# Moving one batch's attention from the first layer's blocks into a phase of the second layer

## The chip, the cores and the metric

One core of one Trainium2 chip. The engines are PE (TensorE, matmuls; PEld is its weight load), DVE (VectorE), ACT (ScalarE), POOL (GpSimd) and SP (SyncE, which issues most DMAs here). The metric is the device time of one execution in microseconds, the median of several.

## The reference

Linear attention with a root-mean-square norm, and two MLPs behind it:

```python
batch, n_heads, seq, head_dim = (8, 8, 576, 64)
kv = np.einsum('bhsd,bhse->bhde', k, v)
out = np.einsum('bhsd,bhde->bhse', q, kv)
rms = np.sqrt(np.mean(out * out, axis=-1, keepdims=True) + 1e-06)
x = out / rms * g_norm                  # to (4608, 512): tokens x (heads * head_dim)
h = x @ w_in                            # (512, 2048)
g = where(h >= 1, h, where(h <= -1, 0, (h + 1) ** 2 / 4))
x = g @ w_out                           # (2048, 512)
h = x @ moe2_w_in
r = np.maximum(h, 0.0)
y = (r * r) @ moe2_w_out
```

## The kernel before

Every fp32 product of the MLPs is made of three matmuls on operands split into a high and a low part (fp32r). Tokens are worked on in blocks of 512, one block for each batch, and the 64 tokens left over of each batch make one block more.

**The plain phase** (to 631 us) does the first layer's blocks 0 to 4 whole and the first contraction of blocks 5 and 6, in steps of one of 16 column groups: `h_stage`, `g_stage` and `out_stage` (`mm3`, L246; activation at L723 and L725). Attention of the later batches is woven into it by `hook(slot, function)`: two slots to a step. For a batch `b` and a pair of heads `hp`, `load_kv` and `load_q` fetch, `kv_stage` makes k'v (`pkv`, L484) and copies it into `kvbd`, `t_stage` transposes q, `o_stage` multiplies (`po`, L588) and squares, and `r_stage` sums the squares (`pr`, L613), forms the reciprocal root on ACT (Ln, Exp, square) and DVE (`newton`, L527) and writes x. `STARTS` gives each pair's slot. The four pairs of batch 7 (`LAST_B`) stand among those of batches 4 to 6; their x is kept in DRAM (`xpd`, `xrd`) for later. Weight preparation is woven in as well: `prep_load`, `prep_narrow`, `prep_join`, `prep_sums`, `prep_split` at the slots of `SECOND` and `FIRSTS`, with the results stored in `wsd`.

**The pair phases** take two blocks at a time through both contractions with seven products in place of eight (`PRODUCTS`, order 1, 6, 2, 7, 5, 4, 3). `PAIRS` lists layer and first block: pair 0 is (layer 1, block 5), pair 1 is (layer 2, block 0), pair 2 is (2, 2), pair 3 is (1, 7), and so on. `in_phase(n)` is pair n's first contraction: four quarters of seven products, 28 steps of 12 matmuls (L924). Product 1 opens accumulators `x`, product 6 `y`, product 5 `z`; products 2, 7, 4 and 3 add onto a bank that has been read before. Banks are read by additions with earlier results, the `e` tiles: product 6 and 7 at L974, products 5, 4 and 3 at L981, with `{5: 7, 4: 1, 3: 6}` naming the `e` tile that each needs. `out_phase(n)` is the second contraction: 56 steps of 6 matmuls, whose operand `prepare` splits into a `t` tile (ACT, then DVE at L853); it reads its banks in the same way. `load_w2` fetches one 512 KB piece of weights for each 12 matmuls, on SP.

Buffers are handed round by `Ring`: a list of (pool, tag) places taken in turn. A tile of a tag waits until one of the tag's buffers has been freed by all who use it. Of those that matter here: tag `g` has three buffers (pool `gp`); `t_ring` is three times `g` and `w0_14`, `w0_15`; `e_ring` is `wk0`, `wk1`, `wk2`, `hl0`, `hl1` and `q`; `ps_ring` are the eight accumulator banks, two `at`, two `h`, four `acc`. Attention uses `at`, `q`, `wk0` to `wk2`, `hl0` and `hl1`.

A finished pair of layer 2 is written by `put_out`, four times, during the next pair's `in_phase`, at its steps 0, 1, 5 and 9 (`late`): DVE transposes (L1131) into a tile `ov` out of `t_ring`, then eight stores on SP (L1119). The order on each engine is set when the program is built: in program order, except that what can't start yet by the builder's own estimate is passed by what can.

Of the kernel before, what the change touches and what calls it, by code (L numbers as in the profile page):

```python
# [76 lines left out]
def linear_attention_rms_two_mlps(  # L77
# [12 lines left out]
    nc = tc.nc  # L90
# [15 lines left out]
    PACE = 0.75  # L106
    WAVE = 6
    WHOLE = ((1, 0), (1, 1))
    STARTS = (32, 39, 46, 53, 60, 66, 72, 78, 84, 90, 96, 102, 109, 115, 121, 127, 133, 139)
    STARTS += (145, 151, 156, 161, 166, 173)  # L110
    SECOND = (38, 47, 55.6, 64.2, 72.8, 84, 92.6, 101.2, 109.8, 119.8, 128.4, 137, 145.6)
    SECOND += (154.2, 166.8, 172.8)
    FIRSTS = (
        (44, 70.2, 78.8, 98.6, 107.2, 134.4, 143, 160.2),
        (81.4, 53, 117.2, 151.6, 90, 61.6, 125.8, 164.2),
    )
    WARMS = ((0, 5), (6, 5), (8, 3), (12, 4), (14, 3), (20, 3), (26, 3))
    SPLITS = (10, 15, 24, 29, 32, 33)
# [20 lines left out]

    PLAIN = 5  # L140
    PAIRS = [(1, PLAIN), (2, 0), (2, 2), (1, B - 1), (2, 4), (2, 6)]
    LAST_B = B - 1

    xpd = dr.tile([P, KD, TB], F32, name="xpd")
# [16 lines left out]
    def keep_halves(L, which, i, n, t, now=False):  # L161

        made = MADE[which][2 * n : 2 * n + 2]
        hs = slice(0, 2)
        if L == 1 and None in made and not (which == 1 and i + n * NH >= NF - TAIL):
            hs = slice(1, 2) if made[0] is None else slice(0, 1)
        dst = wsd[L, which, i // 2][:, 2 * n + hs.start : 2 * n + hs.stop, i % 2]
        if now:
            nc.sync.dma_start(dst, t[:, hs])
        else:  # L170
            owe(2, dst, t[:, hs])
# [15 lines left out]

    def split_halves(t, src, hi, lo):

        src = src.rearrange("p (h f) -> p h f", h=2)  # L190
        copy(hi, t[:, :, 0, :], src)
        lo.tensor_tensor(t[:, :, 1, :], src, t[:, :, 0, :].bitcast(F32), ALU.subtract)  # L192

# [179 lines left out]
    def prep_split(L, which, i, n):  # L373
        src = prep.pop((L, which, i, n))
        t = prep_tile(f"s{L}_{which}_{i}_{n}", [P, 2, 2, H2], F32R)
        split_halves(t, src, engine2("s_hi"), engine2("s_lo"))
        keep_halves(L, which, i, n, t.bitcast(F32))

    def keep_first(which, f):
# [31 lines left out]
    def load_kv(b, hp):  # L411
        h0 = 2 * hp
        if b > 0:

            r = rests[turn[b, hp] % len(rests)]
            kvr[b, hp] = (r[:, 0], r[:, 1])
        for n, src in enumerate((k, v)):
            pool, tag = (ep, "e") if (b, hp) == (0, NP - 1) else (st, "st")
            t = pool.tile([P, TB], F32, tag=tag, name=f"{'kv'[n]}_{b}_{hp}")
            rows = src[b, h0 : h0 + 2, :TB, :].rearrange("h (p r) d -> p h r d", r=MR)  # L420
            if n == 0:

                t = t.rearrange("p (r h d) -> p r h d", h=2, r=MR)
                nc.sync.dma_start(t, rows.rearrange("p h r d -> p r h d"))
            else:
                t = t.rearrange("p (h r d) -> p h r d", h=2, r=MR)
                nc.sync.dma_start(t, rows)
            kvm.setdefault((b, hp), []).append(t)
            if b > 0:
                rest = src[b, h0 : h0 + 2, TB:, :].rearrange("h p d -> p h d")  # L430
                nc.sync.dma_start(kvr[b, hp][n][:REM], rest)
# [169 lines left out]
    def r_stage(b, hp):  # L601
        (y, o), _ = hl.pop((b, hp))
        if (b, hp) in WHOLE:
            products = [(ones.bitcast(F32), y)]
        else:
            products = [(ones, s2) for s2 in og.pop((b, hp))]
        ms = []
        for half in range(2):
            c = slice(half * U, (half + 1) * U)
            ps = bank(b, f"pr_{b}_{hp}_{half}")  # L610
            m = ps[:, :U]
            for n, (one, s2) in enumerate(products):
                nc.tensor.matmul(m, one, s2[:, c], start=n == 0, stop=n == len(products) - 1)  # L613
            nc.scalar.activation(y[:, c], m, AF.Ln, bias=lnb, scale=LN_SCALE)
            ms.append((c, m))
        nc.scalar.activation(y, y, AF.Exp, bias=expb, scale=-0.5)
        t = ap1.tile([P, S], F32, tag="wk2", name=f"t_{b}_{hp}")
        square(engine("y", b), t, y)
        for c, m in ms:
            newton(t[:, c], m)  # L620
        if b < LAST_B:
            norm(t, y, o)
            nc.gpsimd.tensor_copy(xrem[b][:, hp, :], t[:, TB:])
            split(xs[1, b][hp], t[:, :TB], "x", b)
            return
        xt = st.tile([P, TB], F32, tag="st", name=f"xt_{hp}")
        nc.vector.scalar_tensor_tensor(t, t, -3.0, y, op0=ALU.add, op1=ALU.mult)
        nc.vector.tensor_tensor(xt, o[:, :TB], t[:, :TB], ALU.mult)
        xr = ap1.tile([P, REM], F32, tag="xr", name=f"xr_{hp}")
        nc.vector.tensor_tensor(xr, o[:, TB:], t[:, TB:], ALU.mult)  # L630
        x_kept[hp] = xt, xr

    x_kept = {}

    def keep_x(b, hp):
        xt, xr = x_kept.pop(hp)
        nc.sync.dma_start(xpd[:, hp, :], xt)
        nc.sync.dma_start(xrd[:, hp, b, :], xr)

    def new_x(L, b):  # L640
        xs[L, b] = [
# [23 lines left out]
    def attention(starts, order):  # L665

        slots = []
        for j, (s, (b, hp)) in enumerate(zip(starts, order)):
            turn.setdefault((b, hp), len(turn))
            if b == 1:  # L670
                slots += [(max(0, s - 7), load_kv, b, hp), (s, kv_stage, (b, hp))]
            elif j % 2 == 0:
                two = order[j : j + 2]
                turn[two[1]] = len(turn)
                slots += [(max(0, s - 7), load_kv, *i) for i in two]
                slots.append((s, kv_stage, *two))
            slots += [
                (max(0, s - 7), load_q, b, hp),
                (s, t_stage, b, hp),
                (s + 3, o_stage, b, hp, 0),  # L680
                (s + 4, o_stage, b, hp, 1),
            ]
            if hp == 0 and b < LAST_B:
                slots.append((s + 6, begin, b))
            slots.append((s + 6, r_stage, b, hp))
            if b == LAST_B:
                slots.append((s + 8, keep_x, b, hp))
            elif hp == NP - 1:
                slots.append((max(2 * NF * b, 0) if b < PLAIN + 1 else s + 9, store_xrem, b))
        return slots  # L690

# [126 lines left out]
    )  # L818
    e_ring = Ring(*((ap1, t) for t in ("wk0", "wk1", "wk2", "hl0", "hl1")), (ap2, "q"))
    t1_ring = Ring(*[(st, "st")] * 7, (dt, "dt3"))  # L820
    v_ring = Ring(*((wp, f"w0_{i}") for i in (12, 13)))
    tmp = Ring(*[(ep, "e"), (dt, "dt0"), (ep, "e"), (dt, "dt1"), (ep, "e"), (dt, "dt2")])
    ps_ring = Ring(*[(ps_t, "at")] * 2, *[(ps_h, "h")] * 2, *((ps_a, f"acc{c}") for c in range(KD)))
# [96 lines left out]
    def mm_group(ps, lhs, rhs, first, last):  # L920

        for n, (wt, xt) in enumerate(zip(lhs, rhs)):
            for i, (a, c) in enumerate(((0, 0), (0, 1), (1, 0))):
# [6 lines left out]
                    skip_group_check=True,  # L930
                )

    FIRST = (1, 6, 5)
    bank_of = {1: "x", 2: "x", 6: "y", 7: "y", 4: "y", 5: "z", 3: "z"}
    g2 = {}
# [2 lines left out]
    def in_phase(n):  # L938
# [6 lines left out]
        for q in range(NQ):  # L945
            ps = {}
            e = {}
            for p in PRODUCTS:
                w = take_w2(layer(n), 0, q, p)
                for i in range(2):  # L950
# [9 lines left out]
                        True,  # L960
                    )
                    if p == 1:
                        e[i, 1] = tile(e_ring, f"e1_{n}_{k}")
                        g2[k] = [
                            g_ring.tile([P, 2, N], F32, f"g2_{n}_{k}_{j}") for j in range(2)
                        ]
                        nc.scalar.copy(e[i, 1], bank)
                    elif p in (6, 7):
                        kind = "e16" if p == 6 else "e167"
                        if p == 6:  # L970
                            e[i, 6] = tile(e_ring, f"{kind}_{n}_{k}")
                        else:
                            e[i, 7] = tile(e_ring, f"{kind}_{n}_{k}")
                        nc.vector.tensor_tensor(e[i, p], bank, e[i, 1], ALU.add)  # L974
                    else:
                        g = g2[k][0 if p in (2, 3) else 1][:, {2: 0, 3: 1, 4: 0, 5: 1}[p], :]
# [176 lines left out]

    jobs = [(8, store_xrem, 0)]
    jobs += attention((0, 7, 14, 21), [(1, hp) for hp in range(NP)])
    order = []
    for b in range(2, LAST_B):
        order += [(LAST_B, b - 4)] * (b >= 4) + [(b, hp) for hp in range(NP)]
    order.append((LAST_B, NP - 1))
    jobs += attention(STARTS, order)  # L1160
    for job in sorted(jobs, key=lambda j: j[0]):
        hook(*job)
    for i in range(NF):
# [25 lines left out]
    for which in range(2):  # L1189
        for i, t in enumerate(FIRSTS[which]):  # L1190
            parts += [
                (t, prep_join, 1, which, i),
                (t + 1, prep_sums, 1, which, i),
                (t + 1, prep_split, 1, which, i, 2),
                (t + 2, prep_split, 1, which, i, 3),
            ]
    for t, *part in sorted(parts, key=lambda p: p[0]):
        hook(int(t), *part)
# [83 lines left out]
    late = []  # L1282
    rows_left = []

    for n in range(NS + 1):
        step_in = in_phase(n) if n else ()
        for i, _ in enumerate(step_in):
            pay(True)
            if late and i in (0, 1, 5, 9) and n < NS:
                late.pop(0)()  # L1290
# [8 lines left out]
            late.pop(0)()  # L1299
        if n == NS:  # L1300
            break
        result[n] = result_of(dict(g2))
        steps = start_out(n) if n else out_steps[0]
        if n < NS - 1:
            for _ in steps:
                pay(True)
            if n == 0:
                w_ring.slots = [(wp, t) for t in ("w1_14", "w1_15", "w0_0", "w0_1")]
                w_ring.slots += [(wp, f"w1_{i}") for i in range(4)]
# [53 lines left out]
```

## Time and profile before

| what | value |
|---|---|
| median of 3 runs | 1556.14 us (1555.7 to 1557.11) |
| the profiled execution | 1555.4 us |
| its span, first to last instruction | 1553.6 us |
| PE, DVE, ACT busy | 1542.2, 1143.3, 970.6 us |
| matmuls in the trace | 7633 |
| moved by DMA | 369.27 MB, mean 238 GB/s |

The plain phase takes the first 631 us. Pair 0's `out_phase` follows; the `in_phase` of pairs 1, 2 and 3 starts at 707, 860 and 1012 us, each some 76 us long, with an `out_phase` of the same length behind it. Busy time of PE is modelled from pipelined matmuls: a matmul's record is longer than the time until the next one starts, so counts over a stretch say more than durations.

### The profile page before, as it was taken

How to read it: one execution, taken by the hardware profiler on the slowest of the kernel's cores; microseconds unless marked ns; L12 is line 12 of the kernel's file. 1: busy time of each engine (PE TensorE's matmuls, PEld its weight loads, DVE VectorE, ACT ScalarE, POOL GpSimd, SP SyncE). 2: the span in 40 equal slices, each digit the busy share in tenths (PEclk: the TensorE clock that was granted, in tenths of full speed). 3: DMA queues.
4: the chain of work that ended last, by engine and by line, in shares of the span. 5: the costliest groups of instructions: out<-in, count | busy, mean ns of one | idle time of the engine just before them, and what ended most of it. 6: DMA issues, size and time to landing. Idle time of an engine off the chain costs nothing.

```text
span 1553.6 us, 22167 instructions
## 1 busy us (share of the span) xinstructions
PE 1542.2 (99%) x7633; PEld 1273.5 (82%) x7633; DVE 1143.3 (74%) x1991; ACT 970.6 (62%) x1833; POOL 15.1 (1%) x38
## 2 busy tenths in 40 slices
PE   9999999999999999999999999999999999999999
PEld 5787888878878888888888888888888888888899
DVE  6986787787878766984597559778965597558666
ACT  5977676667767667654575466456646664666374
POOL 0000000000000000000000000000000000000000
PEclk9999999999999999999999999999999999999999
DMA  9666899989897945586576867696876676977796
GB/s 290 189 223 187 260 328 292 294 269 289 255 300 214 293 156 179 185 262 216 164 246 197 228 210 248 197 226 212 258 227 205 199 245 196 241 249 213 223 393 249
DMA packets 324479, 369.27 MB, mean 238 GB/s; under 512 B 197008, under 2 KB 222608, under 8 KB 324368
## 3 DMA queue, kind: packets, MB, share of 16 engines
q1 hardware_dynamic: 293472, 311.75, 67.0%
q10 hardware_dynamic: 30896, 56.11, 9.7%
q8 instruction: 61, 1.00, 0.3%
q14 instruction: 50, 0.41, 0.1%
HBM read 283.64 MB, written 84.15 MB: 237 GB/s over the span
## 4 chain that ended last, share of the span: by engine, by line
PE 97%; ACT 1%; DVE 1%; issue 0%; DVEq 0%; ACTq 0%
PE po L924 32%; PE ph L924 27%; PE ph L246 19%; PE acc L246 14%; PE po L588 1%; PE pkv L484 1%; PE pr L613 1%; PE pwarm L1218 1%; ACT raw L276 0%; ACT w L225 0%; PE pr L542 0%; DVE t L527 0%; DVE w L192 0%; PE po L519 0%; ACT u L232 0%; DVE t L530 0%
## 5 line engine op out<-in xcount | busy, mean ns | idle before, releaser
L924 PE MATMUL po<-t,ws 128*128 128x512 f32 x2016 | 458.1, 389 | 0.0
L924 PEld LDWEIGHTS po<-t,ws 128*128 128x128 f32 x2016 | 378.3, 188 | 78.9 <-DVE t L853 0.3
L924 PE MATMUL ph<-x,ws 128*128 128x512 f32 (+1 forms) x2016 | 422.1, 371 | 0.0
L924 PEld LDWEIGHTS ph<-x,ws 128*128 128x128 f32 x2016 | 355.8, 188 | 65.6
L246 PE MATMUL ph<-x,w 128*128 128x512 f32 x1344 | 335.0, 396 | 3.5 <-DVE u L725 2.2
L246 PEld LDWEIGHTS ph<-x,w 128*128 128x128 f32 x1344 | 249.0, 188 | 60.6 <-DVE u L725 4.3
L853 DVE TENSOR_TENSOR t<-g,t 128x512 fp32r<-128x512 f32 (+1 forms) x336 | 216.3, 649 | 91.6 <-ACT t L225 85.8
L225 ACT CAST t<-g 128x512 fp32r<-128x512 f32 (+1 forms) x336 | 195.3, 590 | 119.3 <-PE po L924 60.8
L981 DVE TENSOR_TENSOR h<-ph,e 128x512 f32<-128x512 f32 (+1 forms) x144 | 93.0, 646 | 68.3 <-PE ph L924 60.5
L246 PE MATMUL acc<-gs,w 128*128 128x512 f32 x528 | 134.4, 396 | 1.5 <-DVE u L725 1.5
L246 PEld LDWEIGHTS acc<-gs,w 128*128 128x128 f32 x528 | 97.9, 188 | 22.6 <-DVE u L725 2.0
L246 PE MATMUL acc<-gs,wt 128*128 128x512 f32 x432 | 108.5, 395 | 0.0
L988 ACT ACTIVATE h<-h 128x512 f32<-128x512 f32 (+1 forms) x120 | 70.2, 585 | 60.2 <-DVE h L981 55.3
L974 DVE TENSOR_TENSOR e<-ph,e 128x512 f32<-128x512 f32 (+1 forms) x96 | 61.0, 644 | 51.6 <-PE ph L924 50.8
L246 PEld LDWEIGHTS acc<-gs,wt 128*128 128x128 f32 x432 | 80.3, 188 | 17.0
L725 DVE SCALAR_TENSOR_TENSOR u<-u,ph 128x512 f32<-128x512 f32 x80 | 54.4, 680 | 30.8 <-ACT u L232 30.8
L225 ACT CAST x<-xr 128x512 fp32r<-128x512 f32 (+1 forms) x84 | 48.7, 585 | 43.3 <-DVE xr L904 21.8
L225 ACT CAST gs<-u 128x512 fp32r<-128x512 f32 x80 | 49.8, 622 | 38.6 <-DVE u L725 31.7
L989 ACT ACTIVATE g<-h 128x512 f32<-128x512 f32 (+1 forms) x120 | 70.7, 589 | 3.2
L723 ACT ACTIVATE u<-ph,halfb 128x512 f32<-128x512 f32 x80 | 55.2, 690 | 26.1 <-PE ph L246 21.8
L238 DVE TENSOR_TENSOR gs<-u,gs 128x512 fp32r<-128x512 f32 x80 | 54.9, 686 | 14.6 <-ACT gs L225 14.2
L988 ACT ACTIVATE u<-ph 128x512 f32<-128x512 f32 (+1 forms) x40 | 22.1, 552 | 62.7 <-PE ph L924 61.8
(144 smaller groups left out, 1603.7 us busy)
## 6 DMA issues: line engine op xcount, KB each, us to landing
ws<-wsd SPq DMA_DIRECT2D x364, 512.0 KB, 4.3
wsd<-s ACTq DMA_DIRECT2D x96, 512.0 KB, 4.7
wt<-wsd SPq DMA_DIRECT2D x36, 512.0 KB, 5.6
raw<-in_moe_w_in_dram SPq DMA_DIRECT2D x32, 512.0 KB, 5.9
raw<-in_moe_w_out_dram SPq DMA_DIRECT2D x32, 512.0 KB, 6.6
xr<-x1d SPq DMA_DIRECT2D x36, 256.0 KB, 4.7
out_dram<-ov SPq DMA_DIRECT2D x142, 64.0 KB, 3.8
wsd<-w SPq DMA_DIRECT2D x17, 512.0 KB, 4.6
```

The lines of the kernel that those rows point to most:

```text
L225: return e.copy(dst, src)
L238: lo = engine(op + "_lo", phase).tensor_tensor(t[:, 1, :], src, t[:, 0, :].bitcast(F32), ALU.subtract)
L246: nc.tensor.matmul(dst, wt(a), xt(c), start=first and n == 0, stop=last and n == 2)
L484: nc.tensor.matmul(ps[s, d], lhs, rhs, start=c == 0, stop=c == MR)
L723: nc.scalar.activation(u, ps, AF.Relu, bias=halfb, scale=0.5)
L725: nc.vector.scalar_tensor_tensor(u, u, 1.0, ps, op0=ALU.min, op1=ALU.max)
L853: engine2(op + "_lo").tensor_tensor(t[:, 1, :], src, t[:, 0, :].bitcast(F32), ALU.subtract)
L924: nc.tensor.matmul(ps, wt(a), xt(c), start=first and n == 0 and i == 0, stop=last and n == len(lhs) - 1 and i == 2, skip_group_check=True,)
L974: nc.vector.tensor_tensor(e[i, p], bank, e[i, 1], ALU.add)
L981: nc.vector.tensor_tensor(h, bank, add, ALU.add)
L988: nc.scalar.activation(u, h, AF.Relu)
L989: nc.scalar.activation(g, u, AF.Square)
```

## The change

Batch 7's four pairs leave the plain phase and run in `in_phase(2)`, at its steps 2, 8, 14 and 20 (`in_host`, `host`), their first loads during the `out_phase` before it (negative steps). For that phase `ps_ring` gives up the two `at` banks and gets them back in front of the list behind it; the `e` tiles, two at a time, go to tag `g` (`keep_e`, `e_pairs`) so that attention has `wk*`, `hl*` and `q`; k and v of pairs 2 and 3 go to `w0_14` and `w0_15` (`kv_ring`). x of batch 7 is made in place in `o` and stored at once from there. `STARTS`, `SECOND` and `FIRSTS` are spread anew over the slots. `prep_split` and `keep_halves` leave out weight quarters that no product reads (None in `MADE`).

```diff
-    STARTS = (32, 39, 46, 53, 60, 66, 72, 78, 84, 90, 96, 102, 109, 115, 121, 127, 133, 139)
-    STARTS += (145, 151, 156, 161, 166, 173)
-    SECOND = (38, 47, 55.6, 64.2, 72.8, 84, 92.6, 101.2, 109.8, 119.8, 128.4, 137, 145.6)
-    SECOND += (154.2, 166.8, 172.8)
+    STARTS = (32, 39, 46, 53, 61, 68, 75, 82, 92, 99, 106, 113, 122, 129, 136, 143)
+    STARTS += (151, 156, 161, 166)
+    SECOND = (37, 46, 55.2, 64.6, 73.2, 85, 93.6, 102.2, 110.8, 120.4, 128.8, 137.4, 146)
+    SECOND += (155, 167.6, 173.6)
...
+    HOST = 2
...
-        if L == 1 and None in made and not (which == 1 and i + n * NH >= NF - TAIL):
+        if None in made and not (L == 1 and which == 1 and i + n * NH >= NF - TAIL):
...
-        split_halves(t, src, engine2("s_hi"), engine2("s_lo"))
+        made = MADE[which][2 * n : 2 * n + 2]
+        hs = [h for h in range(2) if made[h]]
+        src = src[:, hs[0] * H2 : (hs[-1] + 1) * H2]
+        split_halves(t[:, hs[0] : hs[-1] + 1], src, engine2("s_hi"), engine2("s_lo"))
...
+        both = None
+        if b == LAST_B and hp > 1:
+            both = kv_ring.tile([P, 2, TB], F32, f"kv_{b}_{hp}")
...
-        xt = st.tile([P, TB], F32, tag="st", name=f"xt_{hp}")
         nc.vector.scalar_tensor_tensor(t, t, -3.0, y, op0=ALU.add, op1=ALU.mult)
-        nc.vector.tensor_tensor(xt, o[:, :TB], t[:, :TB], ALU.mult)
-        xr = ap1.tile([P, REM], F32, tag="xr", name=f"xr_{hp}")
-        nc.vector.tensor_tensor(xr, o[:, TB:], t[:, TB:], ALU.mult)
-        x_kept[hp] = xt, xr
...
+        nc.vector.tensor_tensor(o, o, t, ALU.mult)
+        nc.sync.dma_start(xpd[:, hp, :], o[:, :TB])
+        nc.sync.dma_start(xrd[:, hp, b, :], o[:, TB:])
...
-                (max(0, s - 7), load_q, b, hp),
+                (max(0, s - 7) if b < LAST_B else s - 5, load_q, b, hp),
...
+    kv_ring = Ring(*((wp, f"w0_{i}") for i in (NF - 2, NF - 1)))
+    e_pairs = Ring(*[(gp, "g")] * 3)
+    banks_at = [(ps_t, "at")] * 2
...
+    def keep_e(n, e, i, p, k):
+
+        if n != HOST:
+            e[i, p] = e_ring.tile([P, TB], F32, f"e{p}_{n}_{k}")[:, : width(n)]
+        elif i == 0:
+            t = e_pairs.tile([P, 2, TB], F32, f"e{p}_{n}_{k}")
+            e[0, p], e[1, p] = t[:, 0], t[:, 1]
...
-    order = []
-    for b in range(2, LAST_B):
-        order += [(LAST_B, b - 4)] * (b >= 4) + [(b, hp) for hp in range(NP)]
-    order.append((LAST_B, NP - 1))
-    jobs += attention(STARTS, order)
+    jobs += attention(STARTS, [(b, hp) for b in range(2, LAST_B) for hp in range(NP)])
+    in_host = {}
+    for at, *job in attention((2, 8, 14, 20), [(LAST_B, hp) for hp in range(NP)]):
+        in_host.setdefault(at, []).append(job)
...
+    def host(i):
+        for at in sorted(a for a in in_host if a <= i):
+            for f, *a in in_host.pop(at):
+                f(*a)
...
+        if n == HOST:
+            ps_ring.slots = [a for a in ps_ring.slots if a not in banks_at]
         for i, _ in enumerate(step_in):
+            if n == HOST:
+                host(i)
             pay(True)
             if late and i in (0, 1, 5, 9) and n < NS:
                 late.pop(0)()
...
+        if n == HOST:
+            host(7 * NQ)
+            ps_ring.add(*banks_at)
...
-            for _ in steps:
+            for i, _ in enumerate(steps):
                 pay(True)
+                if n == HOST - 1 and i % 2 == 0:
+                    host(i // 2 - 7 * NQ)
```

## Rows read from the trace of the kernel before

**Rows 1.** The page, busy us of each engine, share of the span, instructions.
```profile
PE 1542.2 (99%) x7633; PEld 1273.5 (82%) x7633; DVE 1143.3 (74%) x1991; ACT 970.6 (62%) x1833; POOL 15.1 (1%) x38
```
**Rows 2.** Windows: PE, PEld, DVE, ACT, POOL busy (count), granted clock, DMA share, GB/s.
```profile
330.00:430.00 100.00, 98.42 (x540) 80.64 (x539) 79.41 (x145) 69.46 (x145) 1.81 (x4) 1.00 0.87 271
430.00:530.00 100.00, 98.89 (x539) 80.64 (x538) 75.37 (x137) 69.10 (x145) 2.09 (x4) 1.00 0.87 269
...
650.00:700.00 50.00, 50.00 (x222) 41.39 (x222) 44.16 (x72) 28.35 (x49) 0.00 (x0) 1.00 0.81 255
...
860.00:936.00 76.00, 76.00 (x337) 62.94 (x336) 43.30 (x66) 44.34 (x74) 0.00 (x0) 1.00 0.78 220
944.00:984.00 40.00, 40.00 (x178) 33.10 (x178) 39.63 (x66) 24.89 (x46) 0.00 (x0) 1.00 0.72 215
```
**Rows 3.** Groups by line, PE, 130 to 631 us: busy, mean ns, idle before, releasers.
```profile
L246 PE MATMUL ph<-x,w 128*128 128x512 f32 x1144 | 284.3, 396 | 2.2 <-DVE u L725 2.2
...
L588 PE MATMUL po<-qT,kvbd 128*128 128x288 f32 x96 | 29.0, 405 | 0.5 <-ACT kvbd L225 0.5
L484 PE MATMUL pkv<-v,k 128*64 128x64 f32 x384 | 15.3, 225 | 0.0
L613 PE MATMUL pr<-s,ones 128*128 128x288 f32 x48 | 14.2, 301 | 0.0
L613 PE MATMUL pr<-s2lo,ones 128*128 128x288 f32 x48 | 11.3, 296 | 0.0
L484 PE MATMUL pkv<-rest 128*64 128x64 f32 x96 | 6.9, 222 | 0.0
```
**Rows 4.** Timeline, 341 to 346 us: start, us, instruction [idle before, its releaser].
```profile
341.85 0.87 ACT L225 COPY kvbd<-pkv 64x64 f32<-64x64 f32 x4 [5.08 <-PE pkv L484]
...
345.94 0.73 PE L246 MATMUL ph<-x,w 128*128 128x512 f32 x2 [1.58 <-DVE u L725]
```
**Rows 5.** Timeline of DVE around the start of the phase that will host.
```profile
854.71 2.67 DVE L1131 STREAM_TRANSPOSE ov<-g 128x512 f32<-128x512 f32 x4
...
869.67 0.69 DVE L974 TENSOR_TENSOR e<-ph,e 128x512 f32<-128x512 f32 x1
```
**Rows 6.** Timeline of PE: first rows of this phase and of the next.
```profile
859.95 2.43 PE L924 MATMUL ph<-x,ws 128*128 128x512 f32 x10
...
936.11 10.14 PE L924 MATMUL po<-t,ws 128*128 128x512 f32 x44
```
**Rows 7.** Timeline of SP's issues, 853 to 900 us.
```profile
855.46 0.69 SPq L1119 DMA_DIRECT2D out_dram<-ov  x1
...
863.25 4.01 SPq L1119 DMA_DIRECT2D out_dram<-ov  x5
...
868.02 5.65 SPq L1119 DMA_DIRECT2D out_dram<-ov  x8
873.77 3.02 SPq L840 DMA_DIRECT2D ws<-wsd  x4
```
**Rows 8.** Tile `ov`, 850 to 905 us: its stores, issue to landing.
```profile
DMA to landing us min/median/max: 2.0/3.9/6.4
```
**Rows 9.** Timeline, 332 to 340 us: the last `pr` of a pair and its `newton`.
```profile
332.08 0.43 PE L613 MATMUL pr<-s2lo,ones 128*128 128x288 f32 x2
...
338.58 0.82 DVE L527 SCALAR_TENSOR_TENSOR t<-pr,t 128x288 f32<-128x288 f32 x2
```
**Rows 10.** Groups by line and form, whole span: `r_stage` behind `pr`.
```profile
L614 ACT ACTIVATE wk<-pr,lnb 128x288 f32<-128x288 f32 x56 | 27.3, 503 | 13.6 <-PE pr L613 13.6
L527 DVE SCALAR_TENSOR_TENSOR t<-pr,t 128x288 f32<-128x288 f32 x64 | 26.4, 452 | 11.7 <-ACT t L232 9.3 <-issue 2.2
...
L616 ACT ACTIVATE wk<-wk,expb 128x576 f32<-128x576 f32 x28 | 22.0, 785 | 0.2
...
L232 ACT ACTIVATE t<-wk 128x576 f32<-128x576 f32 x28 | 19.1, 684 | 0.3
```

More of the change, by code (lines that the diff above doesn't have):

```diff
@@ L108, in linear_attention_rms_two_mlps @@
     WHOLE = ((1, 0), (1, 1))
-    STARTS = (32, 39, 46, 53, 60, 66, 72, 78, 84, 90, 96, 102, 109, 115, 121, 127, 133, 139)
-    STARTS += (145, 151, 156, 161, 166, 173)
-    SECOND = (38, 47, 55.6, 64.2, 72.8, 84, 92.6, 101.2, 109.8, 119.8, 128.4, 137, 145.6)
-    SECOND += (154.2, 166.8, 172.8)
+    STARTS = (32, 39, 46, 53, 61, 68, 75, 82, 92, 99, 106, 113, 122, 129, 136, 143)
+    STARTS += (151, 156, 161, 166)
+    SECOND = (37, 46, 55.2, 64.6, 73.2, 85, 93.6, 102.2, 110.8, 120.4, 128.8, 137.4, 146)
+    SECOND += (155, 167.6, 173.6)
     FIRSTS = (
-        (44, 70.2, 78.8, 98.6, 107.2, 134.4, 143, 160.2),
-        (81.4, 53, 117.2, 151.6, 90, 61.6, 125.8, 164.2),
+        (42.6, 70.2, 78.8, 99.2, 107.8, 134.4, 143, 160.6),
+        (81.4, 52, 117.4, 151.6, 90.6, 60.9, 126, 164.6),
     )
@@ L188, in split_halves @@
     def split_halves(t, src, hi, lo):
-        src = src.rearrange("p (h f) -> p h f", h=2)
+        src = src.rearrange("p (h f) -> p h f", f=H2)
         copy(hi, t[:, :, 0, :], src)
@@ L416, in load_kv @@
             kvr[b, hp] = (r[:, 0], r[:, 1])
+        both = None
+        if b == LAST_B and hp > 1:
+            both = kv_ring.tile([P, 2, TB], F32, f"kv_{b}_{hp}")
         for n, src in enumerate((k, v)):
-            pool, tag = (ep, "e") if (b, hp) == (0, NP - 1) else (st, "st")
-            t = pool.tile([P, TB], F32, tag=tag, name=f"{'kv'[n]}_{b}_{hp}")
+            if both is not None:
+                t = both[:, n, :]
+            else:
+                pool, tag = (ep, "e") if (b, hp) == (0, NP - 1) else (st, "st")
+                t = pool.tile([P, TB], F32, tag=tag, name=f"{'kv'[n]}_{b}_{hp}")
             rows = src[b, h0 : h0 + 2, :TB, :].rearrange("h (p r) d -> p h r d", r=MR)
@@ L625, in r_stage @@
             return
-        xt = st.tile([P, TB], F32, tag="st", name=f"xt_{hp}")
         nc.vector.scalar_tensor_tensor(t, t, -3.0, y, op0=ALU.add, op1=ALU.mult)
-        nc.vector.tensor_tensor(xt, o[:, :TB], t[:, :TB], ALU.mult)
-        xr = ap1.tile([P, REM], F32, tag="xr", name=f"xr_{hp}")
-        nc.vector.tensor_tensor(xr, o[:, TB:], t[:, TB:], ALU.mult)
-        x_kept[hp] = xt, xr
[L633 to L638, printed above, removed]
+        nc.vector.tensor_tensor(o, o, t, ALU.mult)
+        nc.sync.dma_start(xpd[:, hp, :], o[:, :TB])
+        nc.sync.dma_start(xrd[:, hp, b, :], o[:, TB:])
     def new_x(L, b):
@@ L674, in attention @@
                 turn[two[1]] = len(turn)
-                slots += [(max(0, s - 7), load_kv, *i) for i in two]
+                slots += [(s - 7, load_kv, *i) for i in two]
                 slots.append((s, kv_stage, *two))
             slots += [
-                (max(0, s - 7), load_q, b, hp),
+                (max(0, s - 7) if b < LAST_B else s - 5, load_q, b, hp),
                 (s, t_stage, b, hp),
@@ L685, in attention @@
             slots.append((s + 6, r_stage, b, hp))
-            if b == LAST_B:
-                slots.append((s + 8, keep_x, b, hp))
-            elif hp == NP - 1:
+            if b < LAST_B and hp == NP - 1:
                 slots.append((max(2 * NF * b, 0) if b < PLAIN + 1 else s + 9, store_xrem, b))
@@ L962, in in_phase @@
                     if p == 1:
-                        e[i, 1] = tile(e_ring, f"e1_{n}_{k}")
+                        keep_e(n, e, i, 1, k)
                         g2[k] = [
@@ L968, in in_phase @@
                     elif p in (6, 7):
[L969 to L973, printed above, removed]
+                        keep_e(n, e, i, p, k)
                         nc.vector.tensor_tensor(e[i, p], bank, e[i, 1], ALU.add)
@@ L1193, in linear_attention_rms_two_mlps @@
                 (t + 1, prep_sums, 1, which, i),
-                (t + 1, prep_split, 1, which, i, 2),
-                (t + 2, prep_split, 1, which, i, 3),
+                (t + 1.9, prep_split, 1, which, i, 2),
+                (t + 2.8, prep_split, 1, which, i, 3),
             ]
```

## The prediction

> **What bounds the kernel now.** I read the page's totals first, then the busy time by stage, then the matmul engine's idle time by line, then the timeline around its gaps and around the place where the moved work will land. PE is busy for 1542 of 1553.6 us [rows 1]. In the pair phases it never stops: 50 us of a stage with no attention hold 222 matmuls and no idle time, and the hosted phase, the 76 us in which batch 7's attention is to run, is also 76.00 of 76.00 busy [rows 2]. Its clock is granted in full in every stage [rows 2]. So inside those phases no helper engine costs anything; only PE work or a PE wait can. In the plain phase, from 130 to 631 us, PE waits in few places: 2.2 us in front of `ph` and 0.5 us in front of `po` [rows 3], 2.7 us in all. One gap of 1.58 us is behind a late DVE `u` just where an attention chain of ACT, PE and DVE is being worked off [rows 4]. The kernel is therefore at its matmul work, and what a better order of the plain phase can still win is small.
>
> **The attention that moves.** The PE work of a pair of heads is the same wherever it stands. In the plain phase the 24 pairs of batches 2 to 7 cost 15.3 + 6.9 (`pkv`) + 29.0 (`po`) + 14.2 + 11.3 (`pr`) = 76.7 us of PE [rows 3], 3.2 us each. Four pairs leave the plain phase and four enter the hosted one: 12.8 us less there, 12.8 us more here, sum nothing.
>
> **The plain phase without them; preparation spread; quarters not split.** These three only thin out DVE and ACT, which are 79% and 69% busy around the gaps [rows 2]; none removes a matmul. The 16 half splits, the halved `keep_halves` stores and one DVE operation less in `r_stage` of batch 7 are hidden behind PE today, so I put them at nothing by themselves. What all of them can give back together is the idle time: between 0 (the gaps stay, with other waits) and 2.7 us (all gone) [rows 3]. The pairs now start 7 slots apart where many started 6 apart, so I take 2.0.
>
> **A new wait for the `g` buffers.** This is the term that decides. `keep_e` puts the `e` tiles of the hosted phase into tag `g`, of which there are three buffers, and each quarter needs three of them at once: the tile of product 1 lives until product 4 is evicted, that of product 6 until product 3, that of product 7 until product 5. But the finished outputs of the pair before (`put_out`, tiles `ov`) are turned and stored from `t_ring` at that same moment. The ring has five places, the out phase takes 56 tiles from it, so the first two `ov` tiles get `g` as well and the other two get `w0_14` and `w0_15`. The program asks in the order e1, ov0, e6, ov1, e7. Whichever way three buffers are handed out, e7 can be written only when ov0 and ov1 have been transposed, stored in eight DMAs each, and landed. In the kernel before nothing waits for them: product 7's additions write into `ap1` tiles, at 869.67 us [rows 5].
>
> When does that buffer come free? The hosted phase starts at 859.95 us and the out phase behind it at 936.11 [rows 6], so a step (12 matmuls) takes 76.16/28 = 2.72 us. Product 4 is step 5, from 859.95 + 5 × 2.72 = 873.6 us, and its bank must first be read by product 7's addition. Today the first `ov` transposes run at 854.71, as soon as a buffer is free [rows 5]; with e1 ahead of it ov0 gets the next buffer, one out step (1.36 us) later, at 856.0.
> - Least: for each of the two tiles half of the two transposes before the first store can go (0.7 us, since four of 680 ns take 2.67) [rows 5], seven stores issued at 5.65/8 = 0.7 us each [rows 7], 3.9 us from issue to landing [rows 8]: 9.5 us. 856.0 + 2 × 9.5 + 0.69 for the addition is 875.7, so PE waits 2.1 us.
> - Likely: ov0's stores are spaced out by the weight loads between them on SP, as they are today, from 855.46 to 867.26, of which the last starts near 866.5 [rows 7]. Shifted by 1.36 us and with 3.9 to land this is 871.8. ov1 then takes the 9.5 us: 881.3, plus 0.69: 882.0. PE waits 8.4 us. Some of the hosted attention (`po` of the first pair, 29.0/24 = 1.2 us [rows 3]) can be done in it, which leaves 7.2.
> - Most: ov1's stores also stand behind one more group of eight stores and four weight loads (5.65 + 3.02 us [rows 7]): 17 us.
>
> Queued behind it on DVE and ACT is all that evicts this quarter; nothing there is lost beyond PE's wait. On SP stand the weight loads, which wait for PE themselves. I take 7.2 us.
>
> **The other end of the hosted phase.** `banks_at` goes back to the front of `ps_ring`, so the out phase's first two accumulators are the two `at` banks that `r_stage` of the last pair holds, emitted behind step 26. They are free when `newton` has read them. In the plain phase the last `pr` at 332.08 is followed by `newton` ending at 338.58 + 0.82 = 339.40, 7.3 us later [rows 9]; with nothing in between the chain is two Ln, Exp, square and two `newton`, 2 × 0.50 + 0.785 + 0.684 + 2 × 0.45 = 3.4 us [rows 10]. Step 27 covers 2.7 of it. So PE waits between 0.7 and 4.6 us; DVE and ACT are less loaded here (43 and 44 of 76 us [rows 2]) than there, and I take 2.0. The `t` tiles of that out phase can no longer be made early in `g`; DVE is full there for 40 us (39.63 of 40.00 [rows 2]), and this lies in the same wait.
>
> **The rest of the hosted phase.** 24 pairs cost PE 2.7 us of waits in the plain phase, 0.11 each; four cost 0.5. Below: nothing. Above: the largest single gap once for each pair, 6.3 us [rows 4]. I take 0.5. The transfers (k, v, q, and `xpd` now stored from `o`) stay hidden: the hosted phase moves 220 GB/s, the plain phase 271 [rows 2].
>
> **The sum,** against the profiled execution of 1555.4 us: -2.0 + 7.2 + 2.0 + 0.5 = +7.7, 1563.1. The median of the runs shown is 1556.14, 0.7 above that execution, so I predict 1563.8.
>
> **Rivals.**
> 1. The buffers come free in time. For this the two tiles must land before 873 us, under even the least chain above; it could be if the stores go out in a tighter row than any here. Then the plain phase's gain, up to 2.7, stands against the wait at the seam, from 0.7 up: 1553.4 to 1556. Against it: no order of these rows gives it. It decides below 2 us of wait. Chance 0.12.
> 2. Only the least wait: ov0 and ov1 follow each other closely, 2.1 + 2.0 + 0.5 - 2.0 = +2.6, to +4 with a longer seam: 1557 to 1560. For it: SP is fast when nothing stands between (eight in 5.65 us [rows 7]). Chance 0.19.
> 3. The idle engine is clocked down. All gaps in these rows, up to 1.58 us, leave the clock granted in full [rows 2, 4]; what one of 8 us does none shows. At 1.2 GHz instead of 2.4 a step takes 5.4 us instead of 2.7, so each step spent there adds 2.7; with one to two of them, 1566.5 to 1569. Chance 0.12. The Trainium skill, TensorE: Matmul & The Clock Gate, section "Why this matters for your kernels", speaks against this change here: it warns that idle gaps between bursts of matmuls bring the clock back to half. By that rule this third rival would be the likeliest case; the trace before agrees only in that short gaps do not do so.
>
> My own forecast (wait of 4 to 17 us, clock kept) has chance 0.57, its range 1560 to 1573.
>
> **How the numbers follow.** About 0.2%, 3.1 us, is what a measurement of this kernel can tell from no change. Faster by more would need 1553.0 or less, below even rival 1's end: 0.05, from gaps that the modelled matmul ends hide. Same holds the rest of rival 1 (0.07) and two thirds of rival 2 (0.13), 0.20. Slower: 0.75. For the range, leaving out 0.1 on each side: its low end lies within rival 1's upper part, 1555.5; the high end takes in the long wait and the clock's fall in part, 1573.5.
>
> **What will show it.** Right: in the hosted phase PE stands idle at its sixth step, some 14 us in, behind a DVE addition whose own wait ends with an `out_dram<-ov` DMA; the plain phase's 2.7 us shrink; PE waits about 2 us at the following out phase's first `po`, behind `newton`. Wrong: no idle time in that step, or `ov` stores that land before it; then the whole is within 3 us. Also wrong, in size, if the attention that was queued ahead of the addition on DVE stretches the wait, or if the granted clock falls behind the gap.

## The result, and the profile after

The changed kernel takes 1577.55 us (median of 4, 1577.22 to 1577.89) against 1556.34 us for the kernel before (median of 4): 21.2 us more, ratio 1.0137 with a 95% interval of 1.0125 to 1.0149. Slower was forecast, but by 7.7 us, and the time lies above the range.

The stage boundaries say where the time went. Each is a row of PE's timeline of the changed kernel: the first matmul of the out phase behind the plain phase, of the hosted phase, of the out phase behind it, and of the next first contraction. The rows with brackets are all that PE waited for between 840 and 975 us.

```profile
617.27 18.98 PE L926 MATMUL po<-t,ws 128*128 128x512 f32 x83
...
845.75 8.32 PE L926 MATMUL ph<-x,ws 128*128 128x512 f32 x36
...
872.60 18.68 PE L926 MATMUL ph<-x,ws 128*128 128x512 f32 x72 [7.27 <-DVE e L980]
913.91 1.60 PE L598 MATMUL po<-qT,kvbd 128*128 128x288 f32 x4 [3.39 <-DVE qT L571]
919.53 10.95 PE L926 MATMUL ph<-x,ws 128*128 128x512 f32 x36 [4.02 <-DMA ws<-wsd]
953.93 2.11 PE L926 MATMUL po<-t,ws 128*128 128x512 f32 x8 [2.18 <-DVE t L537]
958.04 17.30 PE L926 MATMUL po<-t,ws 128*128 128x512 f32 x68 [1.99 <-DVE t L855]
...
1034.11 4.24 PE L926 MATMUL ph<-x,ws 128*128 128x512 f32 x18
```

The kernel before has the same boundaries at 631.27, 859.95, 936.11 and 1012.27 us; the middle two stand in [rows 6], the others are:

```profile
631.27 4.94 PE L924 MATMUL po<-t,ws 128*128 128x512 f32 x21
...
1012.27 4.01 PE L924 MATMUL ph<-x,ws 128*128 128x512 f32 x17
```

So the plain phase ends 14.0 us sooner; the hosted phase lasts 953.93 - 845.75 = 108.18 us in place of 76.16, 32.0 more; the out phase behind it 80.18, 4.0 more. Together +22.0, which is the difference of the spans (1575.4 and 1553.6) but for 0.2. The plain phase is now without idle time (its 150 to 600 us are 450.00 of 450.00 busy), where [rows 3] had 2.7 us. Of the 36 us lost behind it, 18.85 are the five waits. Some 10 are the attention's own matmuls (worked out below). The rest is the clock. Windows of the changed kernel (columns as in [rows 2]) show PEclk, the granted clock:

```profile
850.00:870.00 20.00, 15.33 (x102) 12.36 (x101) 5.70 (x9) 7.74 (x18) 0.00 (x0) 1.00 0.51 122
870.00:880.00 10.00, 7.40 (x23) 5.96 (x24) 5.30 (x8) 5.88 (x11) 0.00 (x0) 0.66 0.65 156
...
910.00:920.00 10.00, 2.59 (x23) 1.55 (x20) 5.79 (x9) 4.50 (x12) 0.00 (x0) 0.73 0.63 159
920.00:930.00 10.00, 10.00 (x35) 7.93 (x35) 3.46 (x5) 5.32 (x10) 0.00 (x0) 0.76 0.90 274
...
950.00:960.00 10.00, 5.83 (x22) 4.07 (x21) 8.13 (x15) 7.68 (x15) 0.00 (x0) 0.95 0.68 197
960.00:970.00 10.00, 10.00 (x41) 8.18 (x40) 8.58 (x15) 6.28 (x13) 0.00 (x0) 0.88 0.79 247
```

A mean of 0.66 over 10 us is 6.8 us at 1.2 GHz and the rest at 2.4; the three places give 6.8, 10.2 and 3.4 us. In the trace they begin at 870.2, 914.6 and 959.0 us: inside the wait of 7.27 us, between the waits of 3.39 and 4.02, and behind those of 2.18 and 1.99. So 2.4 us of the first lie in the wait that ends at 872.60, and 4.0 of the second in the one that ends at 919.53; those cost nothing. Of the rest half is lost: 2.2 + 3.1 + 1.7 = 7.0 us, an estimate. In [rows 2] the clock was full everywhere.

Who was late? First DVE at the first wait; the rows answer to [rows 5]:

```profile
846.56 0.70 DVE L1137 STREAM_TRANSPOSE ov<-g 128x512 f32<-128x512 f32 x1
...
850.10 0.69 DVE L980 TENSOR_TENSOR e<-ph,e 128x512 f32<-128x512 f32 x1 [0.40 <-PE ph L926]
851.46 0.69 DVE L980 TENSOR_TENSOR e<-ph,e 128x512 f32<-128x512 f32 x1 [0.67 <-PE ph L926]
863.37 0.76 DVE L609 TENSOR_TENSOR s2lo<-wk,s 128x576 fp32r<-128x576 f32 x1 [11.22 <-ACT wk L604]
864.05 1.30 DVE L1137 STREAM_TRANSPOSE ov<-g 128x512 f32<-128x512 f32 x2
867.56 0.82 DVE L537 SCALAR_TENSOR_TENSOR t<-pr,t 128x288 f32<-128x288 f32 x2 [2.21 <-ACT t L233]
...
871.86 1.29 DVE L980 TENSOR_TENSOR e<-ph,e 128x512 f32<-128x512 f32 x2 [1.89 <-DMA out_dram<-ov]
```

The addition at 871.86 is product 7's, on which product 4 waits. It waits for a store of `ov`, as predicted. But the second `ov` tile (864.05) was turned late for another reason than its buffer: it stands on DVE behind `s2lo` of the hosted attention, and DVE had been idle for 11.22 us.

Then SP, to be held against [rows 7]: the stores of the first `ov` tile and, from 892 us, what leads to the wait for `ws`; and the one row of SP's own waits between 880 and 920 us that is longer than 1 us:

```profile
849.08 5.65 SPq L1125 DMA_DIRECT2D out_dram<-ov  x8
...
892.63 2.90 SPq L450 DMA_DIRECT2D q<-in_q_dram  x4
911.27 4.14 SPq L1125 DMA_DIRECT2D out_dram<-ov  x8
915.51 2.57 SPq L842 DMA_DIRECT2D ws<-wsd  x5
```

```profile
SPq L1125 <- DVE ov L1137: 15.7, 1, 15.7
```

From 895.5 to 911.3 us SP issues nothing: next in its queue is a store of the last `ov` tile, which could be written only when `pkv` of the second two pairs had read k and v out of the same place, `w0_15`; DVE turns that tile at 910.54 us. The five weight loads behind that store go out at 915.5, and PE waits for one of them at 919.53.

### The profile page after: what moved, and what is told of

Its sections match the earlier page's. It is cut to its first block, busy times and chain, and to the rows that moved or that the text cites. A ratio compares the mean times of both kernels' runs of the same rounds, so it can differ in the third digit from the quotient of the medians.

```text
span 1575.4 us, 22189 instructions
## 1 busy us (share of the span) xinstructions
PE 1547.7 (98%) x7631; PEld 1278.1 (81%) x7633; DVE 1142.1 (72%) x1987; ACT 971.4 (62%) x1833; POOL 14.8 (1%) x38
## 4 chain that ended last, share of the span: by engine, by line
PE 96%; ACT 2%; DVE 1%; DMA 1%; SPq 0%; issue 0%; DVEq 0%; ACTq 0%
PE po L926 32%; PE ph L926 27%; PE ph L247 18%; PE acc L247 14%; PE po L598 2%; PE pkv L494 1%; PE pr L623 1%; PE pwarm L1223 1%; ACT raw L277 0%; DMA ws<-wsd 0%; ACT w L226 0%; SPq L1125 0%; DMA xr<-xpd 0%; PE pr L552 0%; DVE t L537 0%
## 5 line engine op out<-in xcount | busy, mean ns | idle before, releaser
L926 PE MATMUL ph<-x,ws 128*128 128x512 f32 (+1 forms) x2016 | 430.4, 375 | 11.3 <-DVE e L980 7.3
L247 PE MATMUL ph<-x,w 128*128 128x512 f32 x1344 | 329.9, 395 | 1.3 <-ACT w L226 0.6
```

The costliest lines, as they stand in the source:

```text
L247: nc.tensor.matmul(dst, wt(a), xt(c), start=first and n == 0, stop=last and n == 2)
L926: nc.tensor.matmul(ps, wt(a), xt(c), start=first and n == 0 and i == 0, stop=last and n == len(lhs) - 1 and i == 2, skip_group_check=True,)
```

## The experiments

Theory 1: the waits come from buffers that two users share, `g` (`ov` and `e`) and `w0_14`, `w0_15` (`ov` and k, v). Theory 2: four pairs of heads are too much for DVE, ACT and SP in this phase, whatever the buffers. All ratios are to the kernel before on the same chip, whose medians there were 1555.84 to 1556.27 us.

**All output tiles of pair 1 apart.**

```diff
-        t = (t_ring if n < NS - 1 else v_ring).tile([P, 2, TB], F32, f"ov{n}_{hn}_{hm}")
+        if n == HOST - 1 and True:
+            t_ring.slots.append(t_ring.slots.pop(0))
+            ts = [st.tile([P, TB], F32, tag="st", name=f"ov{n}_{hn}_{hm}_{m}") for m in range(2)]
...
```

`t_ring` is turned by one place for each, so that later tiles keep theirs.

> The changed kernel, with the four output tiles of the pair before (ov, which the hosted phase turns and stores) put into tiles of tag st, where they shared g with the e tiles and w0_14 and w0_15 with k and v. Theory 1 (shared buffers): both stalls of the hosted phase go, 7.27 us in front of ph and 3.39 + 4.02 us in front of po and ph, and with them the stretches at half clock behind them, some 5 us; the seam's 2.18 + 1.99 us stay: 1577.5 - 20 = 1557 to 1558 us. Theory 2 (the attention overloads DVE, ACT and the queue of the hosted phase by itself): the stalls only change their releaser, 1570 to 1577 us.

Measured: 1565.49 us, 1.0060 (1.0046 to 1.0074). The waits behind `e` and `ws` are gone, but others remain:

```profile
883.18 0.75 PE L598 MATMUL po<-qT,kvbd 128*128 128x288 f32 x2 [1.47 <-DVE qT L571]
906.17 2.26 PE L598 MATMUL po<-qT,kvbd 128*128 128x288 f32 x4 [3.49 <-DVE qT L571]
941.79 2.99 PE L926 MATMUL po<-t,ws 128*128 128x512 f32 x8 [2.18 <-DVE t L537]
945.89 29.43 PE L926 MATMUL po<-t,ws 128*128 128x512 f32 x121 [1.11 <-DVE t L855]
```

12 us come back where theory 1 wanted 20. The 3.39 us before `po`, which I had put down to the shared places, is still there as 3.49: theory 1 was wrong on it.

**Only the first two, or only the last two, apart.** The same edit with `hn == 0` in place of `True`, and with `hn == 1`.

> The changed kernel, with only the first two of the four output tiles (those that asked for g) put into st. Theory 1: the wait of 7.27 us behind the e addition goes with its stretch at half clock (some 2.2 us), and the later stalls of 3.39 and 4.02 us behind the last output tiles stay: some 1568 us. Theory 2: the wait stays or moves to another releaser, 1575 to 1578 us.

> The changed kernel, with only the last two of the four output tiles (those that asked for w0_14 and w0_15, where k and v lie) put into st. Theory 1: the loads of ws no longer stand behind stores whose tile waits for k and v, so the stalls of 3.39 and 4.02 us go with the stretch at half clock behind them (some 3.1 us), and the first wait of 7.27 us stays: some 1567 us. Theory 2: these stalls come from the attention's own chain and stay, 1575 to 1578 us.

Measured: 1569.45 us, 1.0087 (1.0073 to 1.0101), and 1569.91 us, 1.0092 (1.0078 to 1.0106). The first takes away the wait behind `e` and leaves 4.51 us behind `ws`; the second takes away that behind `ws` and leaves 7.26 us behind `e`. Each is worth some 8 us, and in the changed kernel either kind of sharing is a cause by itself. In both, the wait before `po` stays (3.39 and 3.49 us).

**The first sharing without any attention.** The kernel before with `keep_e` and `e_pairs` for pair 2.

> The kernel before, with one part of the change alone: the e tiles of this phase go into the three buffers of tag g; no attention is hosted. Theory 1: the wait for the g buffers appears without any attention, 7 to 8.4 us with some 2.2 us for the clock behind it: 1565 to 1567 us. Theory 2: without the attention the output tiles are out in time, 1556 to 1558 us.

Measured: 1557.47 us, 1.0012 (1.0003 to 1.0021): theory 2's number. PE and DVE of this run show why:

```profile
860.46 19.20 PE L926 MATMUL ph<-x,ws 128*128 128x512 f32 x84
880.70 9.59 PE L926 MATMUL ph<-x,ws 128*128 128x512 f32 x41 [1.03 <-DVE e L980]
```

```profile
871.24 1.30 DVE L1137 STREAM_TRANSPOSE ov<-g 128x512 f32<-128x512 f32 x2 [4.37 <-DMA out_dram<-ov]
879.96 1.29 DVE L980 TENSOR_TENSOR e<-ph,e 128x512 f32<-128x512 f32 x2 [7.42 <-DMA out_dram<-ov]
```

The chain of stores is the predicted one, and its ends lie near the forecast: the second tile turned at 871.24 (forecast 871.8), the addition done at 880.65 (882.0). In this there is some luck, since the first tile was turned at 859.30 us, where the forecast had 856.0, and its stores then went faster. But PE has run 84 matmuls, not 60, before it stops: the builder put two steps of the next quarter in front of product 4, as the ring had free banks for them. They hide 5.4 of the 6.5 us.

**The same with two banks less.**

```diff
+        if n == HOST:
+            ps_ring.slots = [a for a in ps_ring.slots if a[1] != "at"]
```

> The run with the e tiles in g without hosted attention, and in addition the two at banks taken out of the ring for this phase, as the change does. With eight banks PE ran 84 matmuls, seven steps, before it stopped for 1.03 us; the last two of them belong to products that come later in the kernel's order. Theory 1 (banks are the cover): with six banks it runs one step less ahead and waits 1.03 + 2.72 = 3.8 us, with up to 2 us for the clock behind it: 1557.5 + 2.7 to 4.7 = 1560 to 1562 us. Rival (banks do not matter here): 1557 to 1558 us.

Measured: 1559.89 us, 1.0023 (1.0014 to 1.0031), with 72 matmuls run before a wait of 2.63 us. The kernel runs one step less ahead, as theory 1 says; the wait is shorter than 3.8 because the addition came 1.13 us sooner (878.83 in place of 879.96), and the clock stayed full. So the banks that the change takes away are a price by themselves: 1.6 us of wait. In the times it is some 2 us (1.0023 against 1.0012), but the two intervals overlap a little.

**One instruction off DVE.** The changed kernel with `s2lo` of the first hosted pair on POOL. Up to 980 us nothing else differs in any engine's order; behind that some neighbours on DVE and ACT change places.

```diff
-            lo = engine("sq_lo", b)
+            lo = nc.gpsimd if (b, hp) == (LAST_B, 0) else engine("sq_lo", b)
```

> The changed kernel with one instruction moved: the s2lo subtraction of the first hosted pair of heads runs on POOL, so that on DVE the two transposes of the second output tile no longer stand behind it (they ran at 864.05 us, 11.2 us after DVE had gone idle). Theory 1a (the shared buffers cost 7.27 us only because the attention stands in front of the output tile on DVE): the second tile is turned at some 857 us, its stores land at 866, the wait shrinks from 7.27 to 1.5 to 2 us, and the stretch at half clock behind it goes: 1577.5 - 5.5 - 2.2 = some 1570 us. Theory 1b (two rounds of stores through one buffer are enough by themselves): the wait stays near 7 us, 1577 us.

Measured: 1576.28 us, 1.0126 (1.0112 to 1.0140), within the interval of the changed kernel and near theory 1b's number; a wait of 5.34 us, which is neither theory's. DVE of this run:

```profile
856.74 1.30 DVE L1137 STREAM_TRANSPOSE ov<-g 128x512 f32<-128x512 f32 x2 [4.31 <-DMA out_dram<-ov]
868.12 0.82 DVE L537 SCALAR_TENSOR_TENSOR t<-pr,t 128x288 f32<-128x288 f32 x2 [10.08 <-ACT t L233]
...
870.45 1.28 DVE L980 TENSOR_TENSOR e<-ph,e 128x512 f32<-128x512 f32 x2
```

The tile is turned at 856.74, as theory 1a says, some 7 us sooner, and the addition no longer waits for its stores. But the addition stands behind the next part of the attention, `newton` of the same pair, for which DVE idles 10.08 us. Theory 1a is right on the tile and wrong on the gain. The queue on DVE is what is late, and the shared buffers are behind its order: with them free from the start (first run) the additions stand at 856.98, ahead of the attention.

**The queries loaded sooner.** The remaining waits before `po` are for `qT`, which stands on DVE behind `newton` of the pair before. The change loads q 5 steps ahead of its turn where the other batches have 7 slots; presumably the builder expects it late and so puts the transpose late (the traces show the order, not the reason). First with the output tiles apart, then with the changed kernel as it is:

```diff
-                (max(0, s - 7) if b < LAST_B else s - 5, load_q, b, hp),
+                (max(0, s - 7) if b < LAST_B else s - 9, load_q, b, hp),
```

> The run with all output tiles apart, and in addition the queries of the hosted pairs loaded nine steps ahead of their turn instead of five, which puts qT on DVE in front of the newton chain of the pair before. Theory 3 (the stalls of 1.47 and 3.49 us in front of po come from qT standing behind that chain): both go, with the 3.4 us at half clock behind them: 1565.5 - 5 - 3.4 = some 1557 us. Theory 2 (four pairs of heads in 28 steps are too much for DVE and ACT whatever their order): another wait of the same size takes their place, 1562 to 1566 us.

> The changed kernel, with only the queries of the hosted pairs loaded nine steps ahead of their turn; the output tiles still share g and w0_14, w0_15. Theory 1 (the shared buffers are the cause, and the order on DVE only follows): the wait behind the e addition stays and grows, since the second output tile now stands behind the first half of newton on DVE (its stores would land near 877 us instead of 871.8, a wait of 11 to 12.5 us); the stall of 3.39 us may go, that of 4.02 us behind the loads of ws stays: 1577 to 1582 us. Rival (the late q is the root of all): 1577.5 - 8 = 1569.5 us.

Measured: 1557.63 us, 1.0010 (1.0001 to 1.0019), and 1574.67 us, 1.0121 (1.0105 to 1.0137). With the tiles apart, both waits for `qT` are gone and 1.31 us stand in their place (0.38 and 0.93); theory 2's wait of the same size does not come. Alone it brings 2.9 us by the medians, with overlapping intervals: the wait behind `e` is now 5.53 us, and two others of 2.73 and 0.81 stand before it, 9.1 in all where I expected 11 to 12.5; the time is some 2 us under the range that I gave for it. The wait for `qT` is gone there too; behind `ws` PE still waits 2.65 us, and 1.98 us before a `pr`. Loading q sooner is no mending without the buffers.

**The seam as well.**

```diff
-            ps_ring.add(*banks_at)
+            t_ring.slots.sort(key=lambda a: a[1] == "g")
+            ps_ring.slots += banks_at
```

The first of the two new lines puts `w0_14` and `w0_15` ahead of the three `g`.

> The run before, and in addition the two at banks put behind the other banks at the end of the hosted phase, and the first two t tiles of the out phase put into w0_14 and w0_15. Theory 1: the seam's 2.18 us behind newton and 1.11 us behind t go with some 1.7 us of half clock behind them: 1557 - 5 = 1552 us, 3 to 4 us below the kernel before by the plain phase's idle time alone. Rival (the plain phase's gain is not real, only moved): 1555.8 us, the kernel before.

Measured: 1554.51 us, 0.9987 (0.9978 to 0.9996), a little faster than the kernel before, but 2.5 us over theory 1's 1552 and nearer to the rival's 1555.8. PE of this run:

```profile
846.27 8.32 PE L926 MATMUL ph<-x,ws 128*128 128x512 f32 x36
...
933.73 4.70 PE L926 MATMUL po<-t,ws 128*128 128x512 f32 x20
939.80 5.51 PE L926 MATMUL po<-t,ws 128*128 128x512 f32 x23 [1.38 <-DVE t L855]
```

`newton` is waited for no more. The wait for `t`, which was to go as well, stays at 1.38 us; moving the `t` tiles brought little. The clock stays full in each window from 850 to 970 us. From 846.27 to 933.73 the hosted phase lasts 87.46 us, 11.3 more than 76.16; less its waits of 1.31 that is 10.0 us of PE for four pairs, the figure used above, 2.5 us a pair.

**The unused quarters alone.** The kernel before with the edits of `keep_halves`, `split_halves` and `prep_split`.

> The kernel before, with one part of the change alone: the quarters of the weights that no product uses are neither split nor stored; times of the units and the attention stay. Theory (as predicted: hidden behind PE, nothing by itself): 1555.8 to 1556.5 us, and the 2.7 us of idle time of the plain phase stay in the profile. Rival (the thinner DVE and ACT are what gives the plain phase's gain back): those 2.7 us go, 1553.5 us.

Measured: 1553.37 us, 0.9985 (0.9977 to 0.9994). The plain phase ends sooner, at 629.70 in place of 631.27 us:

```profile
629.70 6.51 PE L927 MATMUL po<-t,ws 128*128 128x512 f32 x28
```

Its groups from 130 to 631 us have one row with idle time:

```profile
L616 PE MATMUL pr<-s2lo,ones 128*128 128x288 f32 x48 | 12.4, 300 | 2.9 <-DVE s2lo L602 2.8
```

The rival has the time right, and not its reason. The waits of [rows 3] are gone, but a new one of 2.8 us for `s2lo` has come up, so PE shows as much idle time as before, and yet the phase is 1.57 us shorter. Where that comes from is not resolved here.

## Why the prediction was wrong

**The direction was right**, and so were the places of two waits. PE stood idle in the first quarter behind an addition that waits for `out_dram<-ov`, and at the next out phase's first `po` behind `newton`.

**The step that failed is "The rest of the hosted phase",** put at 0.5 us. It is 3.39 + 4.02 = 7.4 us of waits, above its upper bound of 6.3. I costed the attention there by what 24 pairs cost in the plain phase, and did not ask two things that the diff shows: that `kv_ring` takes the very places of the last two `ov` tiles, with the weight loads behind those stores on SP, and that q is loaded only 5 steps ahead. The run with the last two tiles apart (for `ws`) and the one with q loaded sooner and all tiles apart (for `qT`) show each as a cause.

**The clock** was left out of the sum and given a chance of 0.12 as the third rival. It fell at three places and cost about 7 us. The runs bear this out: from the first run to that with q loaded sooner and the tiles apart, the waits between 860 and 960 us fall from 8.25 to 4.61 us, so by 3.6, but the profiled spans by 6.1 (1563.4 and 1557.3; the medians by 7.9). Outside the waits the clock is at half for 11.5 us in the one and 5.3 in the other, which by the same estimate is worth 3.1 us, near the 2.5 that are left. The Trainium skill, TensorE: Matmul & The Clock Gate, section "Why this matters for your kernels", warns of this for idle gaps between bursts of matmuls; the trace after agrees, with granted clocks of 0.66, 0.73, 0.76 and 0.88 in the windows at and behind the waits. I had weighed it by gaps of at most 1.58 us, while forecasting one of 7.2.

**The wait for `g`** measured 7.27 us against 7.2, by luck. Its working had errors of both signs. The stores of the first tile went faster than thought (one row of eight, 5.65 us, in place of twelve microseconds with loads between), and the builder's early step hid 2.72 us. Against that, the first tile was turned at 846.56, 0.8 us behind the start of the phase, where the forecast had it 4 us ahead of the start, and `s2lo` and `newton` of the hosted attention stood ahead of the tile and of the addition on DVE, which the text named only as a doubt at its end.

**The other end** was put at 2.0 us for `newton` and is 2.18; but the `t` tiles, counted into the same wait, are a second one of 1.99 behind it.

**The plain phase** was put at -2.0, at most -2.7. It ends 14.0 us sooner, of which 10.0 are the four pairs, if a pair costs there what it costs in the hosted phase: 4.0 gained. (A pair is 2.5 us by the length of a stage; my 3.2 came from busy times that overlap.) The bound was wrong, since it counted only the idle time that PE's rows show. All 2.7 us of that went, and 1.3 more that no row shows. I had put the unsplit quarters at nothing by themselves; they alone end the phase 1.57 us sooner with as much idle time as before.

Sum as measured: -4.0 + 7.3 + 7.4 + 4.2 + 7.0 = +21.9 against +21.8 in the spans. The whole change with the conflicts taken out that the runs found comes to 1554.5 us, no better than its unsplit quarters alone (1553.4; ratios of 0.9987 and 0.9985): what moving the attention gives the plain phase, the phase that hosts it takes back.

## What to carry to other kernels

When work moves into a phase, list every buffer it takes there and who else holds it at that moment, then follow each engine's queue from the instruction that waits: here a store that waited for k and v held up weight loads, and an output tile stood behind an attention that had nothing to do with it. An order made by a builder's estimates moves with the buffers: taking away one cause on DVE (`s2lo`) let the next one in the queue hold PE for 5.34 us of the 7.27, while freeing the buffers or loading sooner changed the order itself. Where a wait of several microseconds is forecast on a matmul engine, put the slower clock behind it into the sum.

## What was not expected of the hardware

The length of one wait does not tell whether the clock falls. A single wait of 2.63 us (two banks less) left it full, and so did single ones of 1.03 and 1.47 us. With the tiles apart and q loaded sooner, PE waited 1.80 us and, 2.6 us of work later, 1.50. The clock fell at 936.9 us, so 1.4 us behind the first wait and before the second began. PE and its windows there:

```profile
935.49 2.61 PE L926 MATMUL po<-t,ws 128*128 128x512 f32 x8 [1.80 <-DVE t L537]
939.59 5.61 PE L926 MATMUL po<-t,ws 128*128 128x512 f32 x15 [1.50 <-DVE t L855]
```

```profile
925.00:934.00 9.00, 8.69 (x40) 6.89 (x38) 5.75 (x10) 7.93 (x17) 0.00 (x0) 1.00 0.89 325
934.00:944.00 10.00, 7.01 (x19) 5.06 (x20) 8.68 (x15) 6.96 (x13) 0.00 (x0) 0.66 0.80 252
944.00:950.00 6.00, 6.00 (x28) 4.97 (x27) 5.04 (x8) 2.95 (x5) 0.00 (x0) 1.00 0.53 147
```

And with q loaded sooner alone, two waits of 1.72 and 1.99 us at the same place left the clock full:

```profile
952.48 2.11 PE L926 MATMUL po<-t,ws 128*128 128x512 f32 x8 [1.72 <-DVE t L537]
956.58 43.59 PE L926 MATMUL po<-t,ws 128*128 128x512 f32 x191 [1.99 <-DVE t L855]
```

```profile
950.00:960.00 10.00, 6.29 (x27) 4.57 (x26) 8.84 (x16) 8.37 (x16) 0.00 (x0) 1.00 0.84 286
960.00:970.00 10.00, 10.00 (x46) 8.29 (x45) 9.92 (x18) 5.92 (x10) 0.00 (x0) 1.00 0.66 192
```

For the wait of 2.63 us, PE and its window:

```profile
879.58 60.14 PE L926 MATMUL ph<-x,ws 128*128 128x512 f32 x264 [2.63 <-DVE e L980]
```

```profile
870.00:880.00 10.00, 7.37 (x33) 5.82 (x32) 2.47 (x4) 0.09 (x1) 0.00 (x0) 1.00 0.84 195
```

What decides between them is left open.
